# A nested block product moved ahead of attention work in a fused attention and feed-forward kernel

## The chip, the cores and the metric

The kernel runs on one core of a Trainium2 chip. The metric is the device time of one execution in microseconds (us), the median of several; lower is better. The engines are TensorE (PE in the rows; its weight loads are PEld), VectorE (DVE), ScalarE (ACT), GpSimd (POOL) and SyncE (SP, which issues the DMAs).

## The reference

Two branches read the same input x (2048 tokens, width 576) and are mixed by a gate per token. Branch A is causal attention over four segments of 512 tokens with 32 heads of width 18, with a memory read besides. Branch B is a gated feed-forward layer of width 4608.

```
g = sigmoid((x * gate_w).sum(-1, keepdims=True))
a = attention_with_memory(x, wq, wk, wv, wo, beta)   # p = softmax(q k^T scale + mask); o = g_h a_mem + (1-g_h) p v
b = (gelu(x @ w_gate) * (x @ w_up)) @ w_down
return g * a + (1 - g) * b
```

## The kernel before

**Words.** Everything that TensorE multiplies is split into a high and a low float16 word, so one product of two matrices is three matmuls: high by high, high by low, low by high.

**Steps.** After the projections the main part is 72 calls of `step(v)`, v from 0 to 71. The feed-forward width is cut into 36 slices of 128 columns, f = v // 2, and the tokens into two halves, p = v % 2; four steps make a block `fb` of two slices, and `i4 = v % 4` is the place in it. Each step forms the gate and up products of one slice for one half of the tokens. It does so by a fast (Strassen-like) scheme that trades products for sums: `product` (L532) runs one block product of six matmuls of 512 columns into the PSUM banks G (X in the code), U (Y) and V, `rest` (L1302) adds the remaining rows of the width, and VectorE adds or copies between the banks.

**Nesting.** One of these block products, the one into V, is itself split once more into seven smaller products. `nest(at, n)` issues them in four pieces, one step or two ahead of the step that needs them, in the steps with i4 = 3 and i4 = 0. All work on one PSUM bank V with two halves of 256 columns, B and A; a small product is three matmuls of 256 columns (L1376):

- piece 0: a product into B, one into A, then DVE copies A out into `hold` (L1392);
- piece 1: one product into A, then DVE copies A into `hold` (L1395) and B over A (L1396);
- piece 2: one product into B and one into A, then DVE adds A into `hold` (L1400);
- piece 3: one product into A, then DVE adds A into the other half of `hold` (L1403).

Every piece writes a half that DVE has just read, so TensorE waits there for DVE.

**What else a step holds.** `some(fb - 1, ...)` runs down-projection chains of the block before: six matmuls of 288 columns into a bank `dn` (L1256) and one DVE add into `acc` (L1264). `scores(a)` issues the four score matmuls of one head and segment (L1171), of 54 rows of weights each, and `put(a, qi)` has DVE add the mask to one of its four pieces, copy it and find its maximum (L1174). `powers(a)` then computes the exponentials: ACT forms `mb` from the maxima (L1185), four exponentials (L1190) and two copies to float16 (L1191), POOL the low words (L1192), and SP issues two DMA transposes (L1195). `values(a)` multiplies the transposed result by v in 20 matmuls of 37 columns (L1209). `low_rests` adds a leftover of 64 weight rows into G and into U (L1307). `end_first` lets DVE multiply gate and up out of G (`hidden`, L1279); `end_pair` does the same for U at the start of the next step, whose first work on TensorE is `product` into G again. `hidden_pair` (ACT L1286, POOL L1294) splits the outcome into words. The `gl` tiles that hold the gate values have three buffers.

**Order.** The queues of PE, ACT, DVE and POOL carry the instructions in the order in which this code is written. SP's order is set by the scheduler.

Of the kernel before, what the change touches and what calls it, by code (L numbers as in the profile page):

```python
# [43 lines left out]
def kernel(ctx: ExitStack, tc: tile.TileContext, xs, wqk, wv, wo, wgu, wd, beta, out):  # L44
# [8 lines left out]
    def bank(tag, bufs=1, dt=F32):  # L53
        return ps.tile([P, 512 if dt == F32 else 1024], dt, name=tag, tag=tag, bufs=bufs)
# [111 lines left out]
    def fold_squares(c, step):  # L166

        q = x_sq[c]
        if step == 0:
            dve.tensor_tensor(q[:, : 2 * L], q[:, : 2 * L], q[:, 2 * L : 4 * L], OP.add)  # L170
        else:
            dve.tensor_tensor(q[:, L : 2 * L], q[:, L : 2 * L], q[:, 4 * L : 5 * L], OP.add)
            dve.tensor_tensor(q[:, :L], q[:, :L], q[:, L : 2 * L], OP.add)
# [931 lines left out]
    with tc.tile_pool(name="keep", bufs=2, side="right", reuse_waits="tile") as kp, ExitStack() as tail:  # L1105
# [49 lines left out]
        def scored(a, qi):  # L1155
            o = COL[qi]
            t, o = (prob[a][0], o) if o < SPLIT else (prob[a][1], o - SPLIT)
            return t[:, o : o + (qi + 1) * P]
# [20 lines left out]
        def powers(a):  # L1179

            b = ap_.tile([P, 4], F32, name="mb", bufs=2)
            c = 2 * (a // (2 * H)) + a % 2
            h = ap_.tile([P, 10 * P], F16, name="ph", bufs=2)
            t = turned_p[a] = ap_.tile([P, 20, P], F16, name="pt", bufs=2)
            act.activation(b, mx.pop(a), AF.Copy, bias=LN256, scale=esc[:, 1, c : c + 1])  # L1185
            low = prob[a][0].bitcast(F16)
            for i, (p, cols) in enumerate(zip(prob[a], (slice(0, SPLIT), slice(SPLIT, 10 * P)))):
                for qi in ((3, 2), (1, 0))[i]:
                    r = scored(a, qi)
                    act.activation(r, r, AF.Exp, bias=b[:, qi : qi + 1], scale=esc[:, 0, c : c + 1])  # L1190
                act.activation(h[:, cols], p, AF.Copy)  # L1191
                pool.tensor_tensor(low[:, cols], p, h[:, cols], OP.subtract)  # L1192
            prob.pop(a)
            for i, r in enumerate((h, low[:, : 10 * P])):
                sp.dma_start(t[:, 10 * i : 10 * i + 10], r, transpose=True)  # L1195
# [70 lines left out]
        def chains(b, js):  # L1266
            for j in js:
                down(b, j // 2, j % 2)
                if j % 8 == 7:
                    for ff in (2 * b, 2 * b + 1):  # L1270
                        hp.pop((ff, j // 8))
                        hh_free.append(hh_slot.pop((ff, j // 8)))
                        if j == 31:
                            pair_d.pop(ff)
# [98 lines left out]
        def nest_product(b, o, i, j, p, start=False):  # L1373
            w, x = nest_w[b], x_block(p, j)
            for n, (c, d) in enumerate(((0, 0), (0, 1), (1, 0))):
                pe.matmul(o, w[:, (7 * c + i) * P : (7 * c + i + 1) * P], x[d], start=start and n == 0, stop=n == 2,  # L1376
                          skip_group_check=True)

        def nest(at, n):

            if at is None:
                return
            b, p = at
            if n == 0:
                nested[at] = bank("V")
                holds[p] = kp.tile([P, L], F32, name=f"hold{p}", bufs=1)
            B, A = (nested[at][:, i * HX : (i + 1) * HX] for i in range(2))
            h0, h1 = (holds[p][:, i * HX : (i + 1) * HX] for i in range(2))
            if n == 0:
                nest_product(b, B, W00, X00, p, True)  # L1390
                nest_product(b, A, WS3, XT3, p)
                dve.tensor_copy(h1, A)  # L1392
            if n == 1:
                nest_product(b, A, W11, XT4, p)
                dve.tensor_copy(h0, A)  # L1395
                dve.tensor_copy(A, B)  # L1396
            if n == 2:
                nest_product(b, B, W01, X10, p)
                nest_product(b, A, WS2, XT2, p)
                dve.tensor_tensor(h0, A, h0, OP.add)  # L1400
            if n == 3:
                nest_product(b, A, WS1, XT1, p)
                dve.tensor_tensor(h1, A, h1, OP.add)  # L1403
# [6 lines left out]
        def end_first():  # L1410
            hidden(*ends[0])
            ends[0] = ends[0] + (True,)
# [14 lines left out]
        def step(v):  # L1427

            f, p = divmod(v, 2)
            fb, i4 = divmod(v, 4)  # L1430
# [4 lines left out]
            late = range(8 * i4 + 5, 8 * i4 + 8)  # L1435
            some = lambda b, js: chains(b, js) if b >= 0 else None
# [13 lines left out]
            at = (fb + 1, 0) if i4 == 3 and fb + 1 < NB else (fb, 1) if i4 == 0 and fb else None  # L1450
# [130 lines left out]
            if v != 3:  # L1581
                nest(at, 0)
            some(fb - 1, late[:1])
            put(2 * k, 2)
            puts.pop(2 * k, None)
            weights_nest(fb, i4, "late")
            if on(k):
                powers(2 * k)
            if v != 3:
                nest(at, 1)  # L1590
            some(fb - 1, late[1:])
            if on(k - 1):
                values(2 * k - 2)
            if low is not None:
# [1 line left out]
            if fb:  # L1596
                low_rests(f, (X, U4, x1), (Y, UG, x2_))
                ends.append((f, c, X, g0))
                if at:
                    end_first()  # L1600
            if v != 3:
                nest(at, 2)
            if on(k):
                puts[2 * k + 1] = scores(2 * k + 1)
            if v != 3:
# [159 lines left out]
        with tc.manual_schedule(engines=ORDERED):  # L1765
            for v in range(2 * NF):
                step(v)

                if v == LAST:
                    end_pair()  # L1770
                    result_low(H // 2 - 1)
                    atn.close()
                    op_ = tail.enter_context(tc.tile_pool(name="outp", bufs=2, side="right", reuse_waits="tile"))
                if v >= LAST:
                    for _ in range(2):
                        turned(turned_n)
                        turned_n += 1
                if LAST <= v < LAST + 2:
                    finish(v - LAST)
# [3 lines left out]
            fb = NB - 1  # L1783
# [88 lines left out]
```

## Time and profile before

| what | value |
|---|---|
| median of 3 runs | 1576.63 us (1576.33 to 1576.64) |
| profiled execution | 1576.45 us |
| its span, first to last instruction | 1574.7 us |
| PE busy | 1561.6 us, 99% |
| DVE busy | 1248.7 us, 79% |
| ACT busy | 1208.7 us, 77% |
| POOL busy | 1128.9 us, 72% |
| granted TensorE clock, mean | 1.000 |

The busy shares say which engine can be the bound; the table says nothing of waits inside a busy stretch, since the profile lets one matmul overlap the next. For that the timeline's start times have to be read: the time from one start to the next is what a matmul costs in a stream.

### The profile page before, as it was taken

To read this page: it belongs to the slowest core of one execution; us is meant where nothing else is said; L and a number is where in the kernel's file an instruction comes from. 1 tells how busy PE (TensorE), PEld (TensorE's weight loads), DVE (VectorE), ACT (ScalarE), POOL (GpSimd) and SP (SyncE) were. 2 spreads that over 40 slices of the span, in tenths; PEclk is the share of its full clock that TensorE was granted. 3 is DMA by queue.
4 is the path that set the end of the run, shared out by engine and by line. 5 is a ranking of instruction groups with operands and counts; after the bars stand their busy time and mean duration, and the time that the engine had idled before them with its cause. 6 is when DMAs were issued, how large, how long until landed. Compare 5 with 4: busy or idle time off the path is not lost. (4 is left out here: it accounts for less than half of the span.)

```text
span 1574.7 us, 33958 instructions
## 1 busy us (share of the span) xinstructions
PE 1561.6 (99%) x12220; PEld 960.3 (61%) x12220; DVE 1248.7 (79%) x3254; ACT 1208.7 (77%) x2059; POOL 1128.9 (72%) x1220
## 2 busy tenths in 40 slices
PE   9999999999999999999999999999999999999999
PEld 5765655565656666656656565666655666656577
DVE  6878976888787888878787878787888878787565
ACT  7667544888888888888788888888888888887421
POOL 4355565778777868686777777776868687787597
PEclk9999999999999999999999999999999999999999
DMA  6633332567868687777777887878697876764645
GB/s 228 215 125 124 131 118 67 114 126 123 143 125 148 127 145 134 131 134 133 133 127 132 124 147 124 145 126 160 135 127 145 126 140 127 134 112 98 128 86 165
DMA packets 472833, 209.97 MB, mean 133 GB/s; under 512 B 427688, under 2 KB 437416, under 8 KB 472152
## 3 DMA queue, kind: packets, MB, share of 16 engines
q1 hardware_dynamic: 472664, 207.80, 66.5%
q8 instruction: 96, 1.57, 0.4%
q14 instruction: 73, 0.60, 0.1%
HBM read 91.87 MB, written 27.26 MB: 76 GB/s over the span
## 5 line engine op out<-in xcount | busy, mean ns | idle before, releaser
L1192 POOL TENSOR_TENSOR pb<-pb,ph 128x896 f16<-128x896 f32 (+1 forms) x256 | 368.6, 1440 | 248.2 <-ACT ph L1191 237.8
L532 PEld LDWEIGHTS <-pairg 128*128 128x128 f16 x2592 | 248.0, 98 | 258.8 <-issue 12.4
L1256 PE MATMUL dn<-paird,hhr 128*128 128x288 f16 x2115 | 328.7, 286 | 0.1
L1190 ACT ACTIVATE pb<-pb,mb,esc 128x512 f32<-128x512 f32 (+3 forms) x512 | 305.0, 642 | 5.5 <-issue 0.4
L1264 DVE SCALAR_TENSOR_TENSOR acc<-dn,ev,acc 128x288 f32<-128x288 f32 x533 | 262.4, 513 | 32.8 <-PE dn L1256 27.4
L1256 PEld LDWEIGHTS <-hhr 128*128 128x128 f16 x2160 | 207.5, 98 | 78.5 <-issue 11.9
L532 PE MATMUL G<-x,pairg 128*128 128x512 f16 x864 | 209.9, 379 | 1.0 <-DVE gl L1279 1.0
L1256 PE MATMUL dn<-paird,hhd 128*128 128x288 f16 x1275 | 210.1, 286 | 0.2 <-DVE acc L1264 0.2
L532 PE MATMUL U<-xt,pairg 128*128 128x512 f16 x864 | 209.9, 379 | 0.0
L1191 ACT ACTIVATE ph<-pb 128x896 f16<-128x896 f32 (+1 forms) x256 | 188.5, 737 | 8.1
L345 POOL TENSOR_TENSOR pairg<-raw,pairg 128x384 f16<-128x384 f32 (+2 forms) x144 | 157.7, 1116 | 17.8 <-ACT pairg L341 17.8
L1174 DVE CUSTOM_DVE_ANT_0 pb<-st,mask 128x512 f32<-128x512 f32 (+1 forms) x256 | 157.3, 614 | 0.0
L1256 PEld LDWEIGHTS <-hhd 128*128 128x128 f16 x1296 | 124.6, 98 | 50.8 <-issue 7.1
L1174 DVE CUSTOM_DVE_ANT_0 pb<-dn,mask 128x256 f32<-128x256 f32 (+1 forms) x192 | 67.1, 374 | 91.6 <-PE dn L1171 89.9
L1376 PE MATMUL V<-xt,nest 128*128 128x256 f16 x714 | 105.8, 272 | 5.2 <-DVE hold L1400 1.0
L532 PE MATMUL U<-x,pairg 128*128 128x512 f16 x432 | 105.0, 379 | 0.4 <-DVE gl L1552 0.3
L532 PE MATMUL V<-x,pairg 128*128 128x512 f16 x426 | 103.8, 379 | 0.1
L1297 ACT ACTIVATE gl<-gl,sc 128x512 f32<-128x512 f32 x110 | 75.7, 715 | 34.5 <-DVE gl L1552 22.9
L1376 PEld LDWEIGHTS <-nest 128*128 128x128 f16 x714 | 66.8, 97 | 43.4 <-issue 17.0
L1185 ACT ACTIVATE mb<-mx,esc 128x4 f32<-128x4 f32 x128 | 36.8, 288 | 68.6 <-DVE mx L1174 68.6
L1209 PEld LDWEIGHTS <-pt 128*128 128x128 f16 x2560 | 83.4, 96 | 6.3
L1294 POOL TENSOR_TENSOR hhr<-gl,hhr 128x512 f16<-128x512 f32 x64 | 78.1, 1226 | 11.6 <-ACT hhr L1286 11.6
(369 smaller groups left out, 3123.0 us busy)
## 6 DMA issues: line engine op xcount, KB each, us to landing
raw<-in_wgu_dram SPq DMA_DIRECT2D x36, 640.0 KB
rawd<-in_wd_dram SPq DMA_DIRECT2D x36, 288.0 KB
qt<-qk SPq DMA_DIRECT2D x132, 72.0 KB
kt<-qk SPq DMA_DIRECT2D x132, 72.0 KB
qk<-stage SPq DMA_DIRECT2D x36, 256.0 KB
qt<-qk SPq DMA_DIRECT2D x132, 36.0 KB
kt<-qk SPq DMA_DIRECT2D x132, 36.0 KB
vp<-vstage SPq DMA_DIRECT2D x16, 296.0 KB
```

Source lines behind the costliest of these rows:

```text
L345: pool.tensor_tensor(spot(f, *p, 1), raw_g[f][:, p[0] : p[1]], spot(f, *p, 0), OP.subtract)
L532: pe.matmul(o, w[:, i, (a + k) * P : (a + k + 1) * P], x[:, b + k], start=start and k == 0 and i == 0 and b == h, stop=k == 1 and i == 1, ...
L1174: dve.tensor_tensor_reduce(scored(a, qi), out[qi], mask[:, L - (qi + 1) * P :], 1.0, -3e38, OP.add, OP.max, mx[a][:, qi : qi + 1])
L1190: act.activation(r, r, AF.Exp, bias=b[:, qi : qi + 1], scale=esc[:, 0, c : c + 1])
L1191: act.activation(h[:, cols], p, AF.Copy)
L1192: pool.tensor_tensor(low[:, cols], p, h[:, cols], OP.subtract)
L1209: pe.matmul(ov, pr[:, 10 * i + COL[qi] // P + kb], v[:, 4 * e + kb, c0 : c0 + VC], start=kb == 0 and i == 0, stop=kb == qi and i == 1)
L1256: pe.matmul(o[:, :NH], hh[:, a, q * P : (q + 1) * P], w[:, b, n * NH : (n + 1) * NH], start=i == 0, stop=i == 5)
L1264: dve.scalar_tensor_tensor(av, o[:, :NH], ev, av, OP.mult, OP.add)
L1294: pool.tensor_tensor(hh[:, 1], t, hh[:, 0], OP.subtract)
L1297: act.activation(t, o, AF.Gelu_apprx_tanh, scale=scl[f // 2][0][:, 2 + c : 3 + c])
L1376: pe.matmul(o, w[:, (7 * c + i) * P : (7 * c + i + 1) * P], x[d], start=start and n == 0, stop=n == 2, skip_group_check=True)
```

## The change

Piece 1 is now called right after the first of the three late chains, ahead of `put(2 * k, 2)` and of `powers(2 * k)`. Piece 2 is called right behind the other two late chains, ahead of `values`, of `low_rests` with `end_first`, and of `scores(2 * k + 1)`. Pieces 0 and 3 stay. The step v = 3 has its own places and is not touched.

```diff
             some(fb - 1, late[:1])
+            if v != 3:
+                nest(at, 1)
             put(2 * k, 2)
             puts.pop(2 * k, None)
             weights_nest(fb, i4, "late")
             if on(k):
                 powers(2 * k)
+            some(fb - 1, late[1:])
             if v != 3:
-                nest(at, 1)
-            some(fb - 1, late[1:])
+                nest(at, 2)
             if on(k - 1):
                 values(2 * k - 2)
...
                 if at:
                     end_first()
-            if v != 3:
-                nest(at, 2)
             if on(k):
                 puts[2 * k + 1] = scores(2 * k + 1)
```

What this does to the queues is shown at two places. The first is TensorE in a step with i4 = 0, from the last matmul of the late chains to the first product of the next step; bank G is X and bank V the nested one. Before:

```order
L1307 LDWEIGHTS pairg
L1307 MATMUL U<-x_507,pairg 128x512
L1376 LDWEIGHTS nest
L1376 MATMUL V<-xt_2333,nest 128x256 [waits DVE_49]
...
L1171 LDWEIGHTS qt
L1171 MATMUL st<-kt,qt 128x384
...
L1376 MATMUL V<-xt_2333,nest 128x256 [waits DVE_49]
...
L532 MATMUL G<-x_1132,pairg 128x512
```

And of the change:

```order
L1256 MATMUL dn<-paird,hhd_3819 128x288
L1376 LDWEIGHTS nest
L1376 MATMUL V<-xt_2333,nest 128x256 [waits DVE_49]
...
L1307 MATMUL U<-x_507,pairg 128x512
L1171 LDWEIGHTS qt
...
L1171 MATMUL st<-kt,qt 128x384 [waits DVE_49]
...
L1376 MATMUL V<-xt_2333,nest 128x256 [waits DVE_49]
...
L532 MATMUL G<-x_1132,pairg 128x512 [waits DVE_49]
```

The six matmuls of piece 2 now follow the late chains, the scores follow the leftover products (L1307) at once, and the first product into G has a wait for DVE of its own, which it did not have.

The second place is DVE in the same step, from the first copy of the nested bank on:

```order
 L1392 COPY hold_4263<-V 128x256
 L1264 SCALAR_TENSOR_TENSOR acc<-dn,ev,acc 128x288
+L1395 COPY hold_4263<-V 128x256
+L1396 COPY V<-V 128x256
 L1174 ISA pb_4222,mx<-st,mask 128x384
 L1174 ISA mx 128x1
-L1395 COPY hold_4263<-V 128x256
-L1396 COPY V<-V 128x256
```

Piece 1's two copies moved ahead of the score piece (L1174, with its maximum). Further down, the add of piece 2 (L1400) changed places with the multiplication that empties G (L1279). On ACT and POOL nothing moved. On SP the two transposes of `powers(2 * k)` go two loads of the next head (L1128, L1125) further back.

## Rows read from the trace of the kernel before

**Rows 1.** The page, part 1: busy us, share of the span, instructions of each engine.

```profile
span 1574.7 us, 33958 instructions
PE 1561.6 (99%) x12220; PEld 960.3 (61%) x12220; DVE 1248.7 (79%) x3254; ACT 1208.7 (77%) x2059; POOL 1128.9 (72%) x1220
```

**Rows 2.** Instructions of line L1400: count, duration, first and last start.

```profile
L1400 DVE TENSOR_TENSOR hold<-V,hold x34: 415/425/425, 258.3 to 1448.4; 128x256 f32<-128x256 f32 x34
```

**Rows 3.** Timeline of PE, 711 to 717 us (i4 = 0): start us, us, instructions.

```profile
711.86 0.49 PE L1376 MATMUL V<-xt,nest 128*128 128x256 f16 x3
712.18 0.53 PE L1256 MATMUL dn<-paird,hhr 128*128 128x288 f16 x3
...
713.65 0.67 PE L1209 MATMUL pv<-vt,pt 128*128 128x37 f16 x20
714.26 0.39 PE L1307 MATMUL G<-x,pairg 64*128 64x512 f16 x1
...
714.58 0.83 PE L1376 MATMUL V<-xt,nest 128*128 128x256 f16 x6
715.34 0.39 PE L1171 MATMUL st<-kt,qt 54*128 54x512 f16 x2
715.52 0.27 PE L1171 MATMUL dn<-kt,qt 54*128 54x256 f16 x2
715.92 0.49 PE L1376 MATMUL V<-xt,nest 128*128 128x256 f16 x3
716.25 1.46 PE L532 MATMUL G<-x,pairg 128*128 128x512 f16 x6
```

**Rows 4.** Timeline of DVE in the same step; in brackets idle time and what ended it.

```profile
712.05 0.52 DVE L1264 SCALAR_TENSOR_TENSOR acc<-dn,ev,acc 128x288 f32<-128x288 f32 x1 [0.24 <-PE dn L1256]
712.49 0.55 DVE L1174 CUSTOM_DVE_ANT_0 pb<-st,mask 128x384 f32<-128x384 f32 x1
...
712.96 0.42 DVE L1395 COPY hold<-V 128x256 f32<-128x256 f32 x1
713.41 0.43 DVE L1396 COPY V<-V 128x256 f32<-128x256 f32 x1
713.75 0.93 DVE L1264 SCALAR_TENSOR_TENSOR acc<-dn,ev,acc 128x288 f32<-128x288 f32 x2
714.75 0.75 DVE L1279 SCALAR_TENSOR_TENSOR gl<-G,sc,gl 128x512 f32<-128x512 f32 x1
715.45 0.42 DVE L1400 TENSOR_TENSOR hold<-V,hold 128x256 f32<-128x256 f32 x1
716.45 0.42 DVE L1403 TENSOR_TENSOR hold<-V,hold 128x256 f32<-128x256 f32 x1 [0.58 <-PE V L1376]
```

**Rows 5.** Timeline of PE in the step after it (i4 = 1).

```profile
724.91 1.46 PE L532 MATMUL U<-xt,pairg 128*128 128x512 f16 x6
...
732.48 0.66 PE L1209 MATMUL pv<-vt,pt 128*128 128x37 f16 x20
733.07 0.39 PE L1307 MATMUL G<-x,pairg 64*128 64x512 f16 x1
...
733.30 0.38 PE L1171 MATMUL st<-kt,qt 54*128 54x512 f16 x2
```

**Rows 6.** Timeline of ACT, both steps: where `powers` begins.

```profile
713.07 0.30 ACT L1185 ACTIVATE mb<-mx,esc 128x4 f32<-128x4 f32 x1 [2.94 <-DVE mx L1174]
...
732.20 0.30 ACT L1185 ACTIVATE mb<-mx,esc 128x4 f32<-128x4 f32 x1 [1.07 <-DVE mx L1174]
```

**Rows 7.** Timeline of POOL: the low words behind `powers` in that step.

```profile
721.45 1.16 POOL L1294 TENSOR_TENSOR hhd<-gl,hhd 128x512 f16<-128x512 f32 x1
```

**Rows 8.** Timeline of DVE, i4 = 1: the copy that takes the next `gl` buffer.

```profile
722.93 0.69 DVE L1524 COPY gl<-U 128x512 f32<-128x512 f32 x1 [1.64 <-PE U L532]
```

**Rows 9.** Timeline of SP's queue: transposes and the loads behind them.

```profile
718.58 1.41 SPq L1195 DMA_TRANSPOSE pt<-ph  x1
...
721.92 0.48 SPq L1128 DMA_DIRECT2D kt<-qk  x1
```

## The prediction

> **What bounds the kernel now.** I read the page's busy shares first: PE is busy 1561.6 us of a span of 1574.7 [rows 1], so only what moves PE's starts moves the end. Busy time hides small waits, because one matmul overlaps the next. So I then read the timeline of PE start to start in one nested step, and DVE's beside it. Line L1400 runs once in every nested step: 34 times [rows 2]. One of them, v = 3, is not changed, which leaves 33, and the steps from v = 7 on repeat one pattern.
>
> In that pattern PE goes from the late chains to `values` at 713.65, the leftover products (L1307) at 714.26, piece 2 at 714.58, the scores at 715.34, piece 3 at 715.92 and the next step's product into G at 716.25 [rows 3]. Two things in it are not matmul work.
>
> *Changes of row shape.* From the leftover products (64 weight rows) to piece 2 (128 rows) the starts are 0.32 us apart; from leftover products to scores (54 rows), where no nested piece stands between, 0.23 [rows 3, 5]. Six matmuls of piece 2 take 0.76 until the scores start, though three take 0.32 to 0.33 until a chain or the product starts, that is 0.66 for six [rows 3]. Each change between 128 rows and fewer thus costs about 0.10. The step has four: into L1307, out of it, into the scores, out of them.
>
> *A wait for DVE.* Piece 3 starts at 715.92. DVE's add of piece 2 (L1400) ends at 715.45 + 0.42 = 715.87 [rows 4], and 0.05 later PE goes on. DVE in turn came to that add late, since L1279 stood ahead of it, from 714.75 to 715.50.
>
> **What the change takes away.** Piece 2 goes to 713.65, where the chains end. Two of the four changes of shape go with it: chain, piece 2 and `values` all have 128 rows, and the scores follow the leftover products directly. That is 2 x 0.10 = 0.20 a step. The add L1400 has its data 0.9 us sooner and stands ahead of L1279, so piece 3 no longer waits. Without the wait it would start some 0.38 behind the scores: the last two score matmuls start at 715.52, 0.18 in; I add 0.05 for the other's later start, 0.05 for its 128 columns (by the 0.11 of a 256-column matmul, 0.33 / 3) and the 0.10 of the shape. It starts 0.58 behind them now, so 0.20 goes. On PE alone the step would be 0.40 shorter.
>
> **What piece 2 needs in its new place.** B must have been copied over A (L1396). DVE's first add of the step starts at 712.05 and the next instruction 0.44 later [rows 4]. Piece 1 starts at 711.86 and its results are there at 711.86 + 0.49 = 712.35, so L1395 takes the slot of 712.49, and L1396 follows 0.45 behind and ends at 713.37. PE asks for it at 713.65: 0.28 us of cover less 0.05 of signal. If DVE came later than that, piece 2 would wait by the same amount. The score piece then starts at 713.28, and the two adds behind it at 713.75 as before, since the three instructions have only changed places. `dn` thus comes free for the scores as before. I cost the swap on DVE at nothing for PE; the cover is the 0.28.
>
> **What it adds.** The next step's product into G must wait until DVE has emptied G (L1279), and L1279 needs the leftover products, which now stand 0.66 later. Before, this was hidden: L1279 ended at 715.50, and PE came to G at 716.25 with piece 2, scores and piece 3 between [rows 3, 4]. Now scores and piece 3 alone stand between. The chain, all from rows 3 and 4:
>
> - piece 2 starts at 713.65, `values` 0.66 later at 714.31, the leftover products 0.61 later (713.65 to 714.26 now) at 714.92; their results are there 0.39 later, at 715.31;
> - L1279 starts 0.10 behind that, as now (714.26 + 0.39 = 714.65, started 714.75), at 715.41; DVE is free by then: piece 2 ends at 713.65 + 0.83 = 714.48 and L1400 runs behind the two adds, from 714.6 to 715.0;
> - it takes 0.75, to 716.16, and PE goes on 0.05 later: the product into G starts at 716.21.
>
> Now it starts at 716.25. So of 0.40 us won, 0.36 goes into a new wait at the product into G, and 0.04 stays (0.03 to 0.04 by the rounding). The two kinds of nested step (i4 = 3 and 0) have the same distances.
>
> The 0.10 from result to start is the least sure term. L1403 starts 0.04 behind the end of piece 3 (715.92 + 0.49 = 716.41, started 716.45 [rows 3, 4]), and if L1279 did so too, 0.06 more would stay: 0.10 a step. I take the 0.10 because L1279 is the same instruction with the same two waits, for PE and for ACT, and shows it in the row. [...] At the other end, 0.03 more than counted on the chain (a row's rounding three times over) would leave 0.01, and a slightly longer L1279 nothing, or a loss of 0.03.
>
> **What comes later.** The score piece's maximum comes 0.80 us later (L1395 and L1396 stand ahead of it: 712.49 to 713.28). ACT sits idle 2.94 us for it in the step with i4 = 0 [rows 6], so `powers` starts 0.80 later there, and POOL's low words behind it end at 722.61 + 0.80 = 723.41 [rows 7]. The copy L1524 of the next step takes the `gl` buffer that they read; it starts at 722.93 now [rows 8], and would start at about 723.5 and end at 724.2. PE needs U for its next product at 724.91 [rows 5]: 0.7 us of cover. ACT has 1.07 us idle before the next `powers` [rows 6], which takes up the shift. On SP the transposes go two loads back, about half a microsecond each (0.48 for L1128 [rows 9]); their consumer, `values` of the next step, comes at 732.48 [rows 5], 14 us behind the issue at 718.58 [rows 9]. Both cost nothing here.
>
> **Sum.** 33 x 0.04 = 1.2 us (1.0 to 1.3) off the profiled execution's 1576.45 gives 1575.2; the median of the runs lies 0.18 above that execution, so **1575.4 us** against 1576.63. A measurement of this kernel can tell about 0.2%, 3.2 us, from no change. So I forecast no measurable difference.
>
> **Rivals.**
>
> *1. Only the shapes count.* If the new wait at G is no longer than the old one at piece 3 (0.20), the two saved changes stay: 33 x 0.20 = 6.6 us, 1570.0 us. For it: the 0.10 steps in the rows. Against it: the chain above adds up to a wait of 0.36. [...] Chance 0.10.
>
> *2. The wait at G does not bind*, because G is free sooner than I think: all of 0.40 stays, 13.2 us, 1563.4. The listed wait speaks against it, and L1279 would have to take 0.36 less. Chance 0.05.
>
> *3. The short signal.* L1279 starts 0.04 behind the leftover products: 33 x 0.10 = 3.3 us, 1573.3. Chance 0.13, half of it over the 0.2%.
>
> *4. Slower: the late score piece reaches PE.* If `powers` is late by more than the 0.80, POOL's low words hold the `gl` buffer, L1524 comes late and the product into U at 724.91 waits. It decides from 1.5 us of lateness on (0.80 + 0.7). At 1.9 us PE would wait 0.4 in each of 16 blocks: 6.4 us, 1575.4 + 6.4 = 1581.8. For it: ACT's idle time shows that the piece is what `powers` waits for. Against it: nothing but two DVE copies has come between. Chance 0.10.
>
> **How the numbers follow.** The forecast has 0.62. Faster by over 0.2%: 0.10 + 0.05 + half of 0.13 + 0.02 of the forecast's edge, about 0.24; slower by over 0.2%: 0.10 + 0.01 for a chain at G that is longer than counted; the remaining 0.65 is no change. The range leaves out rivals 2 and 4 (0.15): from 1569.8, just under rival 1, to 1577.7, which is the median and 33 x 0.03. The forecast's own range is 1573.3 to 1577.7.
>
> **What would show it.** Right: piece 2 directly behind the chains without a gap, scores 0.23 behind L1307, piece 3 about 0.38 behind the scores, then an idle stretch of some 0.36 us on PE before the product into G, ended by DVE's L1279; ACT idle some 0.8 us longer before `powers` at i4 = 0. Wrong: no such wait (rivals 2 and 3), a wait at piece 2 for L1396, or a wait at the product into U for L1524 (rival 4).

## The result, and the profile after

The changed kernel takes 1581.93 us (median of 6 runs, 1581.35 to 1583.06), the kernel before 1576.24 us beside it (6 runs, 1575.61 to 1576.64). The ratio is 1.0037 with a 95% interval of 1.0024 to 1.005: slower, where no measurable difference was forecast. The profiled execution took 1582.05 us against 1576.45, so it carries the same 5.6 us.

The page of the changed kernel, part 1, answers to [rows 1]:

```profile
span 1580.3 us, 33943 instructions
PE 1560.5 (99%) x12220; PEld 961.0 (61%) x12220; DVE 1253.4 (79%) x3254; ACT 1208.8 (76%) x2059; POOL 1129.8 (71%) x1220
```

PE, DVE, ACT and POOL run as many instructions as before, and PE is busy 1.1 us less, yet the span is 5.6 us longer: PE stands idle more. One busy time has grown that no count explains: DVE's, by 4.7 us with the same 3254 instructions.

**The nested step.** Timeline of PE at the end of the step with i4 = 0, which answers to [rows 3]:

```profile
713.84 0.49 PE L1376 MATMUL V<-xt,nest 128*128 128x256 f16 x3
...
715.63 0.82 PE L1376 MATMUL V<-xt,nest 128*128 128x256 f16 x6
716.28 0.67 PE L1209 MATMUL pv<-vt,pt 128*128 128x37 f16 x20
716.89 0.39 PE L1307 MATMUL G<-x,pairg 64*128 64x512 f16 x1
...
717.11 0.38 PE L1171 MATMUL st<-kt,qt 54*128 54x512 f16 x2
...
717.48 0.50 PE L1376 MATMUL V<-xt,nest 128*128 128x256 f16 x3
718.18 1.46 PE L532 MATMUL G<-x,pairg 128*128 128x512 f16 x6 [0.20 <-DVE gl L1279]
```

Piece 2 follows the chains at once; `values` comes 0.65 behind it, the leftover products 0.61 later, the scores 0.22 after those, and piece 3 0.37 behind the scores. From piece 3 to the product into G it is now 0.70, where it was 0.33 [rows 3]: a new stand of 0.37 us (the time between two starts less what the instructions take in a stream), put down to L1279. From the same product one step earlier (698.60) to this one (718.18) it takes 19.58 us; before it took 19.63 (696.62 to 716.25).

Timeline of DVE in that step, which answers to [rows 4]:

```profile
715.25 0.55 DVE L1174 CUSTOM_DVE_ANT_0 pb<-st,mask 128x384 f32<-128x384 f32 x1
...
717.38 0.75 DVE L1279 SCALAR_TENSOR_TENSOR gl<-G,sc,gl 128x512 f32<-128x512 f32 x1 [0.39 <-PE G L1307]
```

The score piece starts 1.41 behind piece 1 (713.84), before 0.63 [rows 3, 4]: 0.78 later. ACT waits for it, in the row that answers to the first of [rows 6]:

```profile
715.84 0.30 ACT L1185 ACTIVATE mb<-mx,esc 128x4 f32<-128x4 f32 x1 [3.73 <-DVE mx L1174]
```

Idle 3.73 us in place of 2.94.

**Where the time went.** The waits of PE, as a list by place (total us, times, longest us), for the kernel before and then the changed one:

```profile
PE G L532 <- DVE gl L1279: 1.0, 2, 0.6
...
PE dn L1256 <- DVE acc L1264: 0.2, 1, 0.2
```

```profile
PE G L532 <- DVE gl L1279: 8.2, 35, 0.6
PE dn L1256 <- DVE acc L1264: 3.9, 15, 0.3
...
PE dn L1256 <- DVE acc L1262: 1.0, 1, 1.0
```

The first row is the wait that was forecast. The second and the third are new: down-projection chains wait for the add that empties their bank. They stand in the next step, i4 = 1, at the third of the late chains (the expectations of e1 and e3 call it the second). Timeline of PE there, before and after:

```profile
731.34 0.53 PE L1256 MATMUL dn<-paird,hhd 128*128 128x288 f16 x3
731.75 0.53 PE L1256 MATMUL dn<-paird,hhr 128*128 128x288 f16 x3
```

```profile
733.27 0.53 PE L1256 MATMUL dn<-paird,hhd 128*128 128x288 f16 x3
734.09 0.53 PE L1256 MATMUL dn<-paird,hhr 128*128 128x288 f16 x3 [0.28 <-DVE acc L1264]
```

Three such matmuls take 0.37 in a stream. The starts were 0.41 apart, and are 0.82 apart now: the stand grew from 0.04 to 0.45. DVE in the same place, before and after:

```profile
730.43 0.17 DVE L268 TENSOR_REDUCE z<-pv 128x2 f32<-128x10 f32 x1
730.63 0.23 DVE L269 TENSOR_SCALAR z<-x,z 128x4 f32<-128x4 f32 x1
...
731.18 0.52 DVE L1264 SCALAR_TENSOR_TENSOR acc<-dn,ev,acc 128x288 f32<-128x288 f32 x1
```

```profile
732.37 0.16 DVE L268 TENSOR_REDUCE z<-pv 128x2 f32<-128x10 f32 x1
732.56 0.64 DVE L269 TENSOR_SCALAR z<-x,z 128x4 f32<-128x4 f32 x1
...
733.52 0.51 DVE L1264 SCALAR_TENSOR_TENSOR acc<-dn,ev,acc 128x288 f32<-128x288 f32 x1
```

L269, in `scales`, multiplies four numbers per partition. It took 0.23 us and takes 0.64 now, and the add behind it is late by that much. POOL in the same place, before and after:

```profile
728.36 2.04 POOL L345 TENSOR_TENSOR pairg<-raw,pairg 128x384 f16<-128x384 f32 x2
```

```profile
724.21 1.17 POOL L1294 TENSOR_TENSOR hhd<-gl,hhd 128x512 f16<-128x512 f32 x1
...
731.15 2.03 POOL L345 TENSOR_TENSOR pairg<-raw,pairg 128x384 f16<-128x384 f32 x2
```

L345 (`low_g`) is two subtractions that form low words of weights. Measured from the product into G (716.25 and 718.18), L269 starts 14.38 us into the step in both kernels. L345 ended 14.15 us into it (730.40), 0.23 ahead of L269, and ends 15.00 us into it now (733.18), since POOL came late out of the step before. L269 then ends at 733.20, 0.02 behind POOL. And so in all 16 blocks whose sums lie in the bank `pv`, by 0.06 us in one (at 880.15) and by 0.19 to 0.41 in the others; the three L269 outside them take 0.23. The rows of line L269 (min, median, max in ns), before and after:

```profile
L269 DVE TENSOR_SCALAR z<-x,z x19: 229/229/422, 161.5 to 1463.7; 128x4 f32<-128x4 f32 x19
```

```profile
L269 DVE TENSOR_SCALAR z<-x,z x19: 229/633/642, 161.2 to 1469.2; 128x4 f32<-128x4 f32 x19
```

The first block shows it twice. DVE and POOL there, in the changed kernel:

```profile
289.95 0.42 DVE L269 TENSOR_SCALAR z<-x,z 128x4 f32<-128x4 f32 x1
290.29 0.15 DVE L272 TENSOR_SCALAR v<-z 128x2 int32<-128x2 int32 x1
290.40 1.08 DVE L273 TENSOR_SCALAR pb<-z 128x4 int32<-128x4 int32 x1
```

```profile
289.43 0.91 POOL L345 TENSOR_TENSOR pairg<-raw,pairg 128x384 f16<-128x384 f32 x1
...
290.30 1.16 POOL L345 TENSOR_TENSOR pairg<-raw,pairg 128x512 f16<-128x512 f32 x1
```

L269 ends at 290.37, 0.03 behind the first subtraction (290.34); L272 takes its usual 0.15, though by the rows the second has just begun; L273, which takes 0.17 elsewhere, ends at 291.48, 0.02 behind the second (291.46). Here the late chain waits 1.0 us, the L1262 of the list. In the kernel before, the first block had one such hold, the 422 ns of L269's row.

**Account.** A block of four steps (from one product into G behind i4 = 3 to the next) takes 73.62 us in place of 73.30: two nested steps win 0.04 to 0.05 each, the late chain loses 0.41. 15 blocks by 0.32 and 1.0 in the first (L1262) are 5.8 us; the span grew by 5.6.

### The profile page after: what moved, and what is told of

It is laid out like the page before. It is cut to its first block, busy times and chain, and to the rows that moved or that the text cites. A ratio compares the mean times of both kernels' runs of the same rounds, so it can differ in the third digit from the quotient of the medians.

```text
span 1580.3 us, 33943 instructions
## 1 busy us (share of the span) xinstructions
PE 1560.5 (99%) x12220; PEld 961.0 (61%) x12220; DVE 1253.4 (79%) x3254; ACT 1208.8 (76%) x2059; POOL 1129.8 (71%) x1220
## 4 chain that ended last, share of the span: by engine, by line
PE 57%; DVE 6%; POOL 4%; DMA 2%; issue 1%; ACT 0%; SPq 0%; DVEq 0%; ACTq 0%
PE dn L1256 18%; PE U L532 12%; PE G L532 9%; PE V L532 4%; PE V L1376 3%; PE pv L1209 3%; DVE gl L1279 1%; PE U L1302 1%; DVE acc L1264 1%; PE G L1307 1%; PE V L1307 1%; DVE pb L1174 1%; DMA orow<-oa 1%; POOL pairg L1688 1%; PE st L1171 1%; POOL x L1705 1%
## 5 line engine op out<-in xcount | busy, mean ns | idle before, releaser
L345 POOL TENSOR_TENSOR pairg<-raw,pairg 128x384 f16<-128x384 f32 (+2 forms) x144 | 157.8, 1117 | 17.7 <-ACT pairg L341 17.7
L1174 DVE CUSTOM_DVE_ANT_0 pb<-st,mask 128x512 f32<-128x512 f32 (+1 forms) x256 | 157.1, 613 | 1.1 <-DMA pt<-pb 0.9
L1174 DVE CUSTOM_DVE_ANT_0 pb<-dn,mask 128x256 f32<-128x256 f32 (+1 forms) x192 | 67.0, 373 | 92.0 <-PE dn L1171 92.0
```

Source lines behind the costliest of these rows:

```text
L345: pool.tensor_tensor(spot(f, *p, 1), raw_g[f][:, p[0] : p[1]], spot(f, *p, 0), OP.subtract)
L1174: dve.tensor_tensor_reduce(scored(a, qi), out[qi], mask[:, L - (qi + 1) * P :], 1.0, -3e38, OP.add, OP.max, mx[a][:, qi : qi + 1])
```

## The experiments

Theory A: the two copies ahead of the score piece make ACT, then POOL, 0.8 us late at i4 = 0; L345 then overlaps L269, which is held until POOL's running instruction ends; the add behind it, and PE's third late chain, are late. Theory B, the rival: the loss comes with the new wait at G, or with the transposes moved on SP's queue. What each run does to a block, read as above, stands in one table (before: 73.30 us, L269 0.229):

| kernel | block, us | 16 x difference | median, difference to before beside it | L269, median us |
|---|---|---|---|---|
| changed kernel | 73.62 | +5.1 | +5.69 | 0.633 |
| e1 piece 1 only | 73.66 | +5.8 | +6.54 | 0.598 |
| e2 piece 2 only | 73.68 | +6.1 | +5.55 | 0.229 |
| e3 only i4 = 3 | 73.26 | -0.6 | -0.27 | 0.229 |
| e4 scales later | 73.58 | +4.5 | +4.63 | 0.230 |
| e5 POOL longer | 74.10 | +12.8 | +12.21 | 1.042 |
| e6 values last | 73.31 | +0.2 | -0.11 | 0.936 |
| e8 scales in PSUM | 73.39 | +1.4 | +0.44 | 0.225 |
| e9 e3 with values last | 72.96 | -5.4 | -5.45 | 0.229 |
| e10 e8 with values last | 72.80 | -8.0 | -8.44 | 0.225 |

The block explains the time of every run to within about 1 us.

**e1: the copies alone.** Against the changed kernel, piece 2 goes back to its old place; piece 1 stays ahead of the score piece.

```diff
-            if v != 3:
-                nest(at, 2)
             if on(k - 1):
                 values(2 * k - 2)
...
+            if v != 3:
+                nest(at, 2)
             if on(k):
                 puts[2 * k + 1] = scores(2 * k + 1)
```

> Only piece 1 is moved ahead of the score piece; piece 2 stays behind the leftover products. Theory A (the late score piece makes ACT and POOL 0.8 us late at i4 = 0, POOL's low words L345 of the next step then still run when DVE comes to its small L269, which is held until POOL ends; the add L1264 behind it frees a dn bank late and TensorE stands some 0.40 us in the second late chain at i4 = 1): the whole loss is here, without the 0.04 a step that piece 2 brings: 16 x 0.40 = 6.4 us over the kernel before, about 1582.6 us, L269 at about 0.63 us. Theory B (the loss comes from piece 2's new place and the new wait at the product into G): 1576.2 us, L269 at 0.23 us.

Measured: 1582.87 against 1576.33 us, ratio 1.004 (1.0028 to 1.0053). The list of PE's waits:

```profile
PE dn L1256 <- DVE acc L1264: 3.7, 16, 0.2
...
PE G L532 <- DVE gl L1279: 1.0, 2, 0.6
```

No new wait at G, and the whole loss is there with the wait at the late chain. The move of piece 2 is not what costs; the swap on DVE is.

**e3: the new order at i4 = 3 alone.** At i4 = 0 the order is the old one; the calls at both old places get `and i4 != 3`.

```diff
-            if v != 3:
+            if v != 3 and i4 == 3:
                 nest(at, 1)
...
+            if v != 3 and i4 != 3:
+                nest(at, 1)
             some(fb - 1, late[1:])
-            if v != 3:
+            if v != 3 and i4 == 3:
                 nest(at, 2)
...
+            if v != 3 and i4 != 3:
+                nest(at, 2)
```

> The new order in the steps with i4 = 3 alone, the old one at i4 = 0. Theory A (the lateness arises where ACT was idle for the score piece, at i4 = 0): no collision, L269 at 0.23 us, TensorE's stand in the second late chain at i4 = 1 stays at 0.04 us; 16 x 0.04 us gained: 1575.6 us. Theory B (each moved piece 2 costs): about half of the loss, 1579 us. Theory C (the transposes that SP issues behind two loads cost): those still go back at i4 = 3, so some of the loss stays, 1578 us or more.

Measured: 1576.06 against 1576.33 us, 0.9999 (0.999 to 1.0008). The list of waits:

```profile
PE G L532 <- DVE gl L1279: 4.2, 18, 0.6
...
PE dn L1256 <- DVE acc L1264: 0.3, 2, 0.2
```

16 new waits at G, in the same steps the same moves on SP, and no loss. So neither the wait at G nor the transposes that are moved there cost anything by themselves; the loss needs the new order at i4 = 0, just ahead of the step in which `scales` runs. At i4 = 0 SP's order is the old one in this run; e8 below keeps the changed kernel's order there, and all but 0.09 us a block of the loss goes.

**e2: piece 2 alone.** The reverse of e1: piece 2 ahead, the copies of piece 1 behind the score piece as before.

```diff
             some(fb - 1, late[:1])
-            if v != 3:
-                nest(at, 1)
             put(2 * k, 2)
...
                 powers(2 * k)
+            if v != 3:
+                nest(at, 1)
             some(fb - 1, late[1:])
```

> Only piece 2 is moved; piece 1's copies stay behind the score piece, which is thus not late. Theory A: no collision at i4 = 1, L269 at 0.23 us, TensorE's stand in the late chain there back at 0.04. But L1396 ends 0.48 us later than in the changed kernel, so piece 2 waits some 0.24 us at its new place and everything behind it with it: 0.24 less the 0.04 gained is 0.20 in each of 33 steps, 6.6 us, about 1582.8 us. Theory B (piece 2's place alone, without that wait): 1574.9 us.

Measured: 1582.04 against 1576.49 us, 1.0036 (1.0024 to 1.0049). Timeline of PE at i4 = 0:

```profile
714.74 0.53 PE L1256 MATMUL dn<-paird,hhd 128*128 128x288 f16 x3
715.35 0.81 PE L1376 MATMUL V<-xt,nest 128*128 128x256 f16 x6
```

And of DVE:

```profile
714.86 0.43 DVE L1396 COPY V<-V 128x256 f32<-128x256 f32 x1
```

0.61 between the starts where the stream takes 0.37: piece 2 stands 0.24 and starts 0.06 behind the end of L1396 (715.29). A nested step takes 19.82 to 19.83 us in place of 19.63, while L269 stays at 0.229. This is another loss of about the same size: the swap was needed for piece 2, and the 0.28 of cover that the prediction gave it was real.

**e5: POOL longer, in the kernel before.** One subtraction of low words (L1512, 128x512) is done twice at i4 = 1, with the same outcome.

```diff
+                if i4 == 1 and 2 * fb + 1 < NF:
+                    q = parts_g(2 * fb + 1, 1)[1]
+                    pool.tensor_tensor(spot(2 * fb + 1, *q, 1), raw_g[2 * fb + 1][:, q[0] : q[1]],
+                                       spot(2 * fb + 1, *q, 0), OP.subtract)
```

> The kernel before, in its old order, with one of POOL's subtracts (L345) formed a second time at i4 = 1, which lets POOL end some 1.0 to 1.4 us later there; the same result is written again. Theory A: L269 starts while POOL runs and is held until it ends, about 0.8 to 1.2 us against 0.23; the add comes as much later and TensorE stands 0.5 to 1.0 us in each of 16 blocks: 8 to 16 us over the kernel before, 1584 to 1592 us, with no nested piece moved. Theory B: POOL has idle time enough, 1576.2 us.

Measured: 1588.54 against 1576.33 us, 1.0075 (1.0063 to 1.0088). The timelines of POOL, DVE and PE:

```profile
734.29 1.16 POOL L1512 TENSOR_TENSOR pairg<-raw,pairg 128x512 f16<-128x512 f32 x1
```

```profile
734.43 1.04 DVE L269 TENSOR_SCALAR z<-x,z 128x4 f32<-128x4 f32 x1
```

```profile
735.14 0.53 PE L1256 MATMUL dn<-paird,hhd 128*128 128x288 f16 x3
736.35 0.53 PE L1256 MATMUL dn<-paird,hhr 128*128 128x288 f16 x3 [0.68 <-DVE acc L1264]
```

None of the change's moves is in this kernel. L269 starts 0.14 behind POOL's instruction and ends at 735.47, 0.02 after it (735.45), and PE stands 0.84 (1.21 less 0.37). A subtraction on POOL that no row names as PE's releaser costs PE 0.8 us in each block.

**e4: the scales later.** In the changed kernel the instructions of `scales` behind its first sum, and POOL's `scales_out`, go behind the score piece, out of the way of the first add.

```diff
             if fb and i4 == 1:
-                scales(fb + 1, bank("pv") if on(k) else None)
-                scales_out(fb + 1)
+                total = sums(stat[(fb + 1) % 2].rearrange("p a b -> p (a b)"), bank("pv") if on(k) else None)
...
             put(2 * k, 2)
             puts.pop(2 * k, None)
+            if fb and i4 == 1 and on(k):
+                scales_rest(fb + 1, total)
+                scales_out(fb + 1)
```

> The changed kernel, with DVE's chain of small scale instructions at i4 = 1 (L268 to L275) and POOL's that follow it moved behind the down chain's add and the score piece, so that they come when POOL's L345 is over; nothing at the nested steps differs from the changed kernel. Theory A: L269 falls back from 0.63 to 0.23 us, TensorE's stand of 0.44 us in the late chain goes, 16 x 0.40 = 6.4 us come back and the 0.04 of each of 33 steps show: 1574.9 us, faster than both. Theories B and C: 1581.9 us as the changed kernel.

Measured: 1580.96 against 1576.33 us, 1.0029 (1.0017 to 1.0042). A miss: L269 (L271 here, line numbers are 2 higher) is back at 0.230 and the third late chain stands 0.04 again, but only 1 us came back. Timelines of DVE and PE:

```profile
734.68 0.94 DVE L1266 SCALAR_TENSOR_TENSOR acc<-dn,ev,acc 128x288 f32<-128x288 f32 x2
```

```profile
735.32 0.56 PE L1173 MATMUL dn<-kt,qt 54*128 54x256 f16 x2
735.82 1.47 PE L534 MATMUL V<-x,pairg 128*128 128x512 f16 x6
```

The other two adds now stand behind the chain of scales and end at 735.62; the scores write the bank that they empty, and their pair of 0.27 [rows 3] takes 0.56. The experiment took one wait away and made another of 0.3 us. It shows that the collision went, and says nothing of what the time would be without it; for that a run was needed that leaves DVE's order alone (e8).

**e6: values behind piece 3.** In the changed kernel, to take the wait at G away: `values` moves behind piece 3 in the nested steps and covers L1279.

```diff
-            if on(k - 1):
+            if on(k - 1) and (at is None or v == 3):
                 values(2 * k - 2)
...
                 nest(at, 3)
+            if on(k - 1) and at is not None and v != 3:
+                values(2 * k - 2)
```

> The changed kernel, with values moved behind piece 3 in the nested steps, so that its 0.6 us of matmuls stand where TensorE now waits for DVE to empty G. Theory A with the wait at G as predicted: that wait goes (some 0.37 us) in all 33 steps; but at i4 = 0 what TensorE wins there only brings DVE to L269 sooner while POOL's L345 ends when it did, so the stand at the late chain grows by as much there; the win stays at i4 = 3 alone: 1581.9 - 17 x 0.33 = 1576.3 us. If the wait at G were worth nothing: 1581.9. If the collision did not follow POOL's end: 1571.

Measured: 1576.38 against 1576.49 us, 1.0 (0.9991 to 1.0009). Timeline of PE at i4 = 0, and of DVE at i4 = 1:

```profile
714.81 0.67 PE L1209 MATMUL pv<-vt,pt 128*128 128x37 f16 x20
715.33 1.46 PE L532 MATMUL G<-x,pairg 128*128 128x512 f16 x6
```

```profile
729.71 0.94 DVE L269 TENSOR_SCALAR z<-x,z 128x4 f32<-128x4 f32 x1
```

The wait at G is gone and the nested step takes 19.29 us, 0.34 less than before. That brings L269 0.3 sooner against POOL, and it is held 0.3 longer, until 730.65 (L345 starts at 728.59 and ends 2.03 later, at 730.62). What PE gains in two nested steps it stands in the late chain (the third starts 1.11 behind the last matmuls of the second, 730.41 to 731.52, a stand of 0.74): no difference is left.

**e8: the same instruction with one side in PSUM.** In the changed kernel, the small instructions of `scales` write to free columns of the bank that holds the sums, or read from there. The arithmetic is the same, with one small instruction more (7 in place of 6; the parenthesis of the expectation says otherwise and is wrong). Line numbers are higher by up to 13: L272 is the former L269, L358 the former L345.

```diff
+        if bk is not None:
+            zp, tp = bk[:, 16:20], bk[:, 20:22]
+            dve.tensor_scalar(zp, x2, z[:, 4:5], 1e-30, OP.mult, OP.max)
...
+            dve.tensor_scalar(pb[:, 0].bitcast(I32), zp.bitcast(I32), EXP, None, OP.bitwise_and)
```

> The changed kernel, its order kept, with each of DVE's small scale instructions at i4 = 1 reading from or writing to PSUM, so that none both reads and writes SBUF (one small instruction more is not needed: the two results of each pair are formed from the one in PSUM). Theory A in its sharp form (DVE and POOL exclude each other where a DVE instruction goes from SBUF to SBUF): L269 takes 0.2 us although L345 runs, the chain L268 to L275 takes about 0.75 to 0.95 us, TensorE's stand in the late chain falls from 0.44 to 0.04 to 0.2 us: 1575 to 1578 us. Theory A in a loose form (any small DVE instruction is slow while POOL runs): L269 stays at 0.6 us, 1581.9 us.

Measured: 1576.93 against 1576.49 us, 1.0005 (0.9996 to 1.0014). Timelines of POOL, DVE and PE in one block:

```profile
876.49 2.04 POOL L358 TENSOR_TENSOR pairg<-raw,pairg 128x384 f16<-128x384 f32 x2
```

```profile
877.71 0.16 DVE L269 TENSOR_REDUCE z<-pv 128x2 f32<-128x10 f32 x1
877.91 0.23 DVE L272 TENSOR_SCALAR pv<-x,z 128x4 f32<-128x4 f32 x1
...
878.65 0.51 DVE L1277 SCALAR_TENSOR_TENSOR acc<-dn,ev,acc 128x288 f32<-128x288 f32 x1
```

```profile
878.62 0.53 PE L1269 MATMUL dn<-paird,hhr 128*128 128x288 f16 x3
879.21 0.53 PE L1269 MATMUL dn<-paird,hhd 128*128 128x288 f16 x3
```

POOL is as late as in the changed kernel, its instruction runs until 878.53, and the multiplication starts and ends within it in its usual 0.23 us (225 ns in all 16). So neither a semaphore nor POOL's lateness as such holds L269: with SBUF on both sides it took 0.633 us in the changed kernel (median), with PSUM on one side it takes 0.225. What stays is the longer chain, 0.94 from its reduction (L269 here, L268 before) to the add in place of 0.75, and a stand of 0.22 in place of 0.04: that is why 0.09 a block is still lost.

**e9 and e10: what the change could have been.** e9 is e3 with `values` behind piece 3 at i4 = 3; e10 is e8 with `values` behind piece 3 in both nested steps. What e9 adds to e3 (e10 adds the same to e8, without the conditions on `i4`):

```diff
-            if on(k - 1):
+            if on(k - 1) and (at is None or v == 3 or i4 != 3):
                 values(2 * k - 2)
...
                 nest(at, 3)
+            if on(k - 1) and at is not None and v != 3 and i4 == 3:
+                values(2 * k - 2)
```

> The new order and values behind piece 3 at i4 = 3 alone; at i4 = 0 the order of the kernel before. Theory A: no score piece is late where ACT idles for it, so no collision; at i4 = 3 the wait at the product into G is covered by values: 0.33 to 0.37 us in each of 16 steps, with what e3 gave, 1570 to 1571 us, faster than both kernels. If DVE or POOL give it back later in the block: 1576 us.

Measured for e9: 1571.04 against 1576.49 us, 0.9966 (0.9953 to 0.9978).

> Both remedies on the changed kernel: the scale instructions through PSUM and values behind piece 3 in all nested steps. Theory A: the stand of 0.73 us that values behind piece 3 alone left at the late chain (i4 = 1) falls to the 0.22 us that the PSUM chain alone showed: 1576.4 - 15 x 0.51 = 1568.7 us; from the other side, 1576.9 - 33 x 0.30 = 1567.0 us. If what TensorE wins at i4 = 0 is eaten by another wait on ACT or POOL, which run 0.8 us late there: 1572 us or more.

Measured for e10: 1567.78 against 1576.22 us, 0.9946 (0.9933 to 0.996). Both are faster than the kernel before beside them and than the changed kernel's 1581.93, and both came out as the terms add up: 0.34 a nested step won once the wait at G is covered, 0.18 a block lost to the longer chain of scales in e10.

## Why the prediction was wrong

**Right: the nested step.** Every distance was met within 0.02 us: the two changes of shape gone, L1279 0.10 behind its data (716.89 + 0.39 = 717.28, start 717.38), the wait at G of 0.36 (0.37), the win of 0.04 a step (0.04 to 0.05). The choice of the 0.10 over the 0.04 signal was right, so rival 3 falls; rivals 1 and 2 fall with the wait. The trace of the kernel before lists an instruction at L1279 that only waits for a semaphore (0.02 us, 70 times), and none at L1403, which goes with the two waits at L1279 on which the prediction rested the 0.10. The swap gave piece 2 its data in time, and e2 shows what it would have cost without.

**Right: the lateness.** 0.80 us for the score piece (0.78), and as much for ACT's `powers` (0.79). Two slips in the prediction's sums change nothing: 712.49 to 713.28 is 0.79, and 33 x 0.04 is 1.3.

**Wrong: the step "What comes later", "Both cost nothing here".** It followed the lateness to the waits that it could see, the `gl` buffer of L1524 and ACT's 1.07 us of idle time. Three things in it failed.

- The slack that takes up the shift comes too late. ACT's 1.07 us stand at 732.20 [rows 6]; POOL carries the lateness through L345, which before ended at 730.40, ahead of that.
- The cover that decided was not the 0.7 us at L1524 but 0.23 us, from the end of L345 to the start of L269. No semaphore ties the two, so no wait in the kernel before names them. Its trace did hold a sign: the longest L269 took 422 ns against a median of 229.
- The price was therefore not nothing but 0.41 us a block: 15 blocks of that and the 1.0 of the first are 7.2 us, against the 1.3 won.

**Rival 4** had the sign, the first links (late score piece, ACT, POOL, DVE, PE) and by chance the size, 1581.8 us. Its place was wrong. L1524 starts 6.68 us behind the product into G in both kernels (722.93 less 716.25 [rows 3, 8], 724.86 less 718.18), the second time before POOL's hhd ends (724.21 + 1.17 = 725.38): the buffer it takes is not the one that POOL still reads. Its threshold of 1.5 us of lateness is wrong with it; 0.23 was enough. The 0.10 given to it rested on "nothing but two DVE copies has come between", which is just what made 0.78 us.

What the prediction left out, the rows show: where L269 started while a POOL subtraction ran, it took 0.64 us (changed kernel), 0.94 (e6) and 1.04 (e5), until 0.02 to 0.03 behind the end of that subtraction, and 0.225 with PSUM on one side (e8). These runs show the hold and what ends it; what in the two engines makes the one wait for the other, no row shows.

## What to carry to other kernels

When a change makes an engine late, list what it then overlaps, not only who waits for it: here L269, a VectorE instruction of 0.23 us with SBUF on both sides, took 1.04 us while a GpSimd subtraction ran, and ended 0.02 behind it (e5). Look for the distance between the end of a long GpSimd instruction and the next such VectorE instruction (0.23 us here), and for a longest duration well above the median of one line (0.42 against 0.23 us in the kernel before). With one side in PSUM L269 took 0.225 us within the subtraction (e8), and a wait that a reorder uncovers can be paid with independent work moved behind it, as `values` did here (0.34 us a nested step in e6).

## What the runs showed of the hardware

A VectorE instruction on 128x4 numbers, from SBUF to SBUF, took 0.17 us (L273) or 0.23 us (L269) alone and up to 1.21 us (the longest L269 of e1); where the rows show one held, it ended 0.02 to 0.03 us behind a GpSimd subtraction.

Not everything on VectorE is held. The reduction ahead of it (L268), which reads PSUM, took 0.16 us within GpSimd's instruction and 0.17 outside. Nor is every instruction with SBUF on both sides: in the kernel before, during the projections, the reciprocal L732 (128x32) ran from 207.98 for its usual 0.35 us while L345 ran from 207.03 until 209.06, and the multiplication right behind it (L733, also 128x32 in SBUF) took 0.74 us in place of 0.19, until 209.11. So an operation has to be looked up in a trace before it is counted as held or as free.

In these rows a hold ends with the GpSimd instruction that runs when the VectorE instruction starts. In the first block of the changed kernel L269 came 0.39 us before the end of the first subtraction and was out 0.03 behind it, although the second had just begun. The 1.21 us of e1 is longer than the 1.16 us of one such subtraction and 0.03; whether a second one took that hold over, no row here shows. What happens the other way round, a GpSimd instruction that comes while such a VectorE instruction runs, no run here was made to show.
